# A planned order of instructions: statistics spread out, the last PSUM bank opened to dense groups, projections due earlier

## The chip, the core and the metric

The kernel runs on one core of a Trainium2 chip. Its time is device microseconds of one launch. Five engines take part: PE (matmul), ACT, DVE and POOL (element-wise work), and SP, which here only starts transfers. Each runs its own instructions in the order in which they were written; what one needs from another it waits for.

## The reference

Two kinds of layer alternate, A, B, A, B, each added to its input, on x of 2048 rows by 512 columns in bfloat16. Both A layers use the same weights, and so do both B layers.

```python
def _A_ref(x, wqkv, wo):
    H = 32; Dh = D // H; W = 256
    qkv = (x @ wqkv).reshape(B, S, 3, H, Dh)          # then q, k, v
    scores = einsum("bhqd,bhkd->bhqk", q, k) * (Dh ** -0.5)
    mask = (idx[:, None] - idx[None, :] >= 0) & (idx[:, None] - idx[None, :] < W)
    p = softmax(where(mask, scores, -1e9))
    o = einsum("bhqk,bhkd->bhqd", p, v)
    return o.transpose(0, 2, 1, 3).reshape(B, S, D) @ wo

def _B_ref(x, w1, w2):
    return maximum(x @ w1, 0) @ w2                    # Dff = 1792

x = A_x
x = x + _A_ref(layernorm(x), A_wqkv, A_wo)
x = x + _B_ref(layernorm(x), B_w1, B_w2)
x = x + _A_ref(layernorm(x), A_wqkv, A_wo)
x = x + _B_ref(layernorm(x), B_w1, B_w2)
```

So: 32 heads of 16 channels, attention over a window of 256 rows back, and a two-matrix block with relu.

## The kernel before

**Tiling.** The 2048 rows are cut into four chunks of 512 rows. A step k is one chunk of one pair of layers (A then B): k = 0 to 3 are the four chunks of the first pair, 4 to 7 of the second, and the texts below count chunks by this k. Step k does, in this order of data: statistics and normalising of x (`norm_stats`, `norm_pow`, `norm_apply`; the tile xn), a transpose to xnT, projections to K, Q and V, attention, a transpose of its output O to OT, the product with wo, the sum into x_sb, a second norm to xn2T, the product with w1 and relu to hT, the product with w2 and the sum. Transposes are DMA transposes on SP's queue, except those of the first and the last step, which PE makes.

**Projections.** K is spread with a zero for every other head into KBD (`spread_k`, two instructions per group), Q is copied to Qt, V is copied to Vst and then spread into V2f (`spread_v`, four instructions), in which a column of ones gives the softmax's sum. The zeros and ones of V2f are written once at the start (`c_v0` on POOL, `c_v` on DVE), the zero pads between the tiles of Pb as well (`pads`).

**Attention.** Units of 32 channels and up to eight blocks of 64 queries are cut into score groups. Each group is a set of small matmuls into the one score tile Sps (four banks), an exponential on ACT from there into Pb, and masks on POOL (two `affine_select` per block) or DVE (a minimum with `tri`). Then PV matmuls accumulate into acc, and DVE divides (a reciprocal and a product). Sps has one copy, so the scores of a group wait for the exponential of the group before.

**PSUM.** Four of the eight banks belong to Sps. The other four (the pool `psum`) are shared by the dense groups (projections, wo, w1, w2, made by `group`), by acc, by the PE transposes and by filler matmuls.

**The order of the work.** Nothing is ordered by hand. While the program is built, every piece is an `Op` with a key, a duration guessed for each engine that may do it, and what it depends on. A list scheduler (lines 686 to 786) plays these durations through: whenever an engine is free it takes the ready op of the lowest key (on the other engines than PE, of the lowest time of readiness plus key), books a buffer if the op needs one, and writes the instructions. What is written stays in that order on each engine (`InOrder`). The guessed durations set the order and nothing else; the chip takes its own time.

- Transfers of x and weights are ops that end at a fixed guessed time (`landed`, lines 235 to 238).
- A key of -1e5 + s ranks the score group s first on PE, -5e4 the PV groups, -10000 the product with wo; projections have as key the number of the first score group that needs them, less `wait` (line 484), and w1 and w2 the number of a later one.
- `keep` (lines 270 and 711): a dense group of key above -9000 may start only while more than one bank is free.
- Statistics have key 0 (line 280), so DVE takes them in the order in which x lands.
- When PE has nothing to do, a filler matmul on `ident` (the tile `warm`, lines 774 to 783) is written, if more than one bank is free.

After the loop stands an exact path for sums out of range, which a check at the end of the main path skips for these inputs.

Of the kernel before, what the change touches and what calls it, by code (L numbers as in the profile page):

```python
# [9 lines left out]
FP32 = mybir.dt.float32  # L10
# [3 lines left out]
ACT = mybir.ActivationFunctionType  # L14
# [48 lines left out]
def kernel(  # L63
# [32 lines left out]
    class InOrder:  # L96


        def __init__(self, eng):
            self.eng, self.last = eng, None  # L100

        def __getattr__(self, op):
            fn = getattr(self.eng, op)

            def call(*a, **k):
                inst = fn(*a, **k)  # L106
                if chained[0]:
# [143 lines left out]
    EVAC = {512: {"DVE": 0.66, "ACT": 0.59}, 256: {"DVE": 0.42, "ACT": 0.38}}  # L251
# [4 lines left out]
    def group(key, n, us, make, deps=(), item_deps=None, width=512, lead=0):  # L256

        box = Box(psum)
        box.ps = None
        last = None  # L260
        for i in range(n):
            def fn(i=i):
                if i == 0:
                    box.ps = box.tile([P, 512], FP32, "ps_d")
                make(i, box.ps)
            d = list(deps) if i == 0 else [last]
            if item_deps is not None:
                d.append(item_deps[i])
            last = op(key if i == 0 else key - lead, {"PE": (us, fn)}, d, box if i == 0 else None, [box],
                      1 if key > -9000 else 0)  # L270
        return box, last

    def norm_stats(lid, j, src, deps, eps_from=None):
        def fn():
            st = small.tile([P, 6], FP32, name="st", bufs=4)
            dve.bn_stats(out=st[:], in_=src)
            dve.bn_aggr(out=mvs[:, lid % 8, j, :], in_=st[:])
            if eps_from is not None:
                dve.tensor_scalar_add(rstds[:, lid % 8, eps_from:j + 1], mvs[:, lid % 8, eps_from:j + 1, 1], 1e-5)
        return op(0, {"DVE": (0.85 + (0.16 if eps_from is not None else 0), fn)}, deps)  # L280
# [5 lines left out]
    def norm_apply(lid, j, src, deps, by_array, dst, then_key, dst_deps):  # L286
# [12 lines left out]
        times = {"DVE": 0.46} if by_array else {"POOL": 1.15, "DVE": 0.5}  # L299
        a = op(0, options(times, fn), list(deps) + list(dst_deps), box)  # L300
# [8 lines left out]
    def transpose(key, src, dst, deps, uses, take=None):  # L309
        box = Box(psum)  # L310

        def fn():
            box.ps = box.tile([P, KC, P], BF16, "tp")
            for kc in range(KC):
                pe.transpose(box.ps[:, kc, :], src()[:, kc * P:(kc + 1) * P], ident[:])
        t = op(key, {"PE": (0.26, fn)}, deps, box, list(uses) + [box])
        return op(0, options({"DVE": 0.6, "ACT": 0.59}, lambda e: copy(e, dst(), box.ps[:])), [t], take, [box])
# [120 lines left out]
    c_v0 = [op(6, {"POOL": (0.96, lambda s0=s0: pool.memset(V2f[:, 544 * s0:544 * (s0 + 4)].bitcast(FP32), 0.0))})  # L438
# [5 lines left out]
    c_v = [op(12, {"DVE": (0.6, lambda s0=s0: v_ones(s0))}, [c_v0[s0 // 4]]) for s0 in range(0, NSLOT, 4)]  # L444
# [16 lines left out]
    def plan_qkv(k):  # L461
# [22 lines left out]
        wait = 0 if k == 0 else 8  # L484
        for h in range(2) if k == 0 else (None,):
# [5 lines left out]
            for t in range(4):  # L491
# [6 lines left out]
                times = {"DVE": 1.42, "ACT": 1.37} if h is None else {"DVE": 0.82, "ACT": 0.76}  # L498
# [15 lines left out]
        for j in range(4):  # L514
# [11 lines left out]
            v_done[k, j] = op(at, options({"POOL": 1.65, "DVE": 1.42} if k else {"POOL": 1.65, "DVE": 1.42, "ACT": 1.48}, lambda e, j=j, vs=vs: spread_v(e, layer, c, j, vs.t[:])),  # L526
# [3 lines left out]
    def plan_attention(k):  # L530
        layer, c = divmod(k, NCH)
        prev = units_of.get(k - 1, []) if c else []
        for n in units_of[k]:
# [3 lines left out]
            for g in range(len(u.groups)):  # L537
# [17 lines left out]
                for m in u.masks(g):  # L555
                    times = {"DVE": 0.32 + 0.14 * (len(m) - 1), "POOL": 0.88 * len(m)}
                    masks[s].append(op(0, options(times, lambda e, m=m, g=g, pb=pb: mask(e, m, places(pb, g))), [exps[s]] + c_tri))
            for jl in range(u.nq // 2):
# [24 lines left out]
                divs[k, u.t, j] = op(-1, {"DVE": (0.46, dfn)}, [pvs[n, jl]] + war + checks[k - 2:k - 1], None, [box])  # L583
        checks.append(op(40, {"DVE": (1.5, lambda k=k: accumulate_check(chks[k % 2], k == 0))},
# [121 lines left out]
    score_next = [0]  # L706

# [21 lines left out]
    def begin(e, t, o):  # L729
# [7 lines left out]
        us, fn, *total = o.opts[e]  # L737
        fn()
# [204 lines left out]
```

## Time and profile before

| | |
|---|---|
| runs | 504.32, 506.89, 507.78 us; median 506.89 |
| the profiled execution | 508.45 us, its span 506.4 us |
| mean granted clock of PE | 0.978 |
| busy: PE, DVE, ACT, POOL | 465.0, 363.5, 345.4, 303.0 us |
| first projection starts | 11.32 us |
| last matmul group | up to 500.8 us, then a sum on DVE and the last store |

Line numbers in the profile are nearly all L106, because every instruction passes through the helper `InOrder`; groups are told apart by their tiles. In the names, `ps_d<-xnT,wqkv` is a projection to K or Q, `ps_d<-wqkv,xnT` one to V, `ps_d<-wo,OT` the product with wo, `ps_d<-xn2T,w` and `ps_d<-w,hT` those with w1 and w2, `Sps<-Qt,KBD` scores, `acc<-V2f,Pb` PV, `tp` a transpose on PE. PEld is PE's loading of weights, which lies beside its matmuls. A bracket at the end of a row of the timeline gives the idle time of the engine before the row and what ended it.

### The profile page before, as it was taken

To read this page: it belongs to the slowest core of one execution; us is meant where nothing else is said; L and a number is where in the kernel's file an instruction comes from. 1 tells how busy PE (TensorE), PEld (TensorE's weight loads), DVE (VectorE), ACT (ScalarE), POOL (GpSimd) and SP (SyncE) were. 2 spreads that over 40 slices of the span, in tenths; PEclk is the share of its full clock that TensorE was granted. 3 is DMA by queue.
4 is the path that set the end of the run, shared out by engine and by line. 5 is a ranking of instruction groups with operands and counts; after the bars stand their busy time and mean duration, and the time that the engine had idled before them with its cause. 6 is when DMAs were issued, how large, how long until landed. Compare 5 with 4: busy or idle time off the path is not lost.

```text
span 506.4 us, 14630 instructions
## 1 busy us (share of the span) xinstructions
PE 465.0 (92%) x5989; PEld 253.8 (50%) x6064; DVE 363.5 (72%) x977; ACT 345.4 (68%) x298; POOL 303.0 (60%) x681
## 2 busy tenths in 40 slices
PE   8669899999799998999998999998999899999995
PEld 3335555655455543554444455554454554455662
DVE  5878886978778885798757976888558883586411
ACT  2747787878578876786667877886677767665340
POOL 6658866658786487646735657767547663563000
PEclk9769999999899999999999999999999999999999
DMA  8903112112130022203202201211202202000000
GB/s 268 350 8 60 25 24 23 22 24 44 23 63 3 12 46 31 43 3 43 43 1 43 43 14 32 43 13 33 53 29 48 43 3 64 23 1 13 32 22 27
DMA packets 54651, 22.00 MB, mean 43 GB/s; under 512 B 46128, under 2 KB 54064, under 8 KB 54576
## 3 DMA queue, kind: packets, MB, share of 16 engines
q1 hardware_dynamic: 54576, 20.98, 18.7%
q8 instruction: 49, 0.80, 0.7%
q14 instruction: 26, 0.21, 0.1%
HBM read 7.86 MB, written 2.10 MB: 20 GB/s over the span
## 4 chain that ended last, share of the span: by engine, by line
PE 66%; POOL 11%; DVE 6%; DMA 6%; ACT 5%; issue 4%; SPq 1%; POOLq 0%; ACTq 0%; DVEq 0%
PE ps_d L106 46%; PE acc L106 12%; PE Sps L106 8%; POOL Pb L106 6%; ACT Pb L106 4%; DMA xnT<-xn 3%; DMA x_sb<-in_A_x_dram 2%; POOL rstds L106 2%; DVE st L106 1%; POOL xn L106 1%; POOL V2f L106 1%; DVE KBD L106 1%; SPq L106 1%; DVE Pb L106 1%; DMA xn2T<-xn 1%
## 5 line engine op out<-in xcount | busy, mean ns | idle before, releaser
L106 ACT ACTIVATE Pb<-Sps 128x2048 bf16<-128x2048 f32 (+4 forms) x164 | 283.9, 1731 | 107.8 <-PE Sps L106 77.6
L106 POOL TENSOR_SCALAR_AFFINE_SELECT Pb<-Pb 64x256 bf16<-64x256 bf16 x502 | 219.5, 437 | 136.2 <-ACT Pb L106 115.5
L106 PE MATMUL ps_d<-xn2T,w 128*128 128x512 bf16 (+1 forms) x540 | 107.9, 335 | 2.4 <-issue 1.4
L106 PE MATMUL ps_d<-w,hT 128*128 128x512 bf16 x426 | 105.1, 382 | 1.7 <-issue 1.0
L106 PEld LDWEIGHTS <-Pb 128*128 128x128 bf16 x2880 | 84.8, 96 | 32.7 <-issue 9.7
L106 PE MATMUL acc<-V2f,Pb 128*128 128x34 bf16 x2880 | 91.6, 179 | 8.2 <-DVE V2f L106 4.0
L106 DVE TENSOR_TENSOR Pb<-Pb,tri 128x512 bf16<-128x512 bf16 (+1 forms) x140 | 58.6, 423 | 24.8 <-ACT Pb L106 24.1
L106 PE MATMUL Sps<-Qt,KBD 32*128 32x192 bf16 (+4 forms) x1536 | 62.8, 250 | 10.7 <-ACT Pb L106 6.1
L106 PE MATMUL ps_d<-xnT,wqkv 128*128 128x512 bf16 (+1 forms) x268 | 66.3, 367 | 4.3 <-DMA xnT<-xn 2.9
L106 PEld LDWEIGHTS <-w 128*128 128x128 bf16 x560 | 50.8, 97 | 38.3 <-issue 4.4
L106 PEld LDWEIGHTS <-hT 128*128 128x128 bf16 x448 | 40.5, 98 | 45.2 <-issue 3.2
L106 PEld LDWEIGHTS <-KBD 32*128 32x128 bf16 x1536 | 27.1, 92 | 58.2 <-issue 50.0
L106 DVE TENSOR_SCALAR hT<-ps_d 128x512 bf16<-128x512 f32 (+1 forms) x79 | 48.7, 622 | 8.3 <-PE ps_d L106 7.4
L106 DVE BATCH_NORM_STATS2 st<-x_sb 128x6 f32<-128x512 f32 (+1 forms) x64 | 43.8, 684 | 5.2 <-DMA x_sb<-in_A_x_dram 4.6
L106 DVE TENSOR_TENSOR x_sb<-ps_d,x_sb 128x512 f32<-128x512 f32 x48 | 32.6, 685 | 15.8 <-PE ps_d L106 15.7
L106 DVE RECIPROCAL chk<-acc 128x8 f32<-128x8 f32 x128 | 26.0, 203 | 24.3 <-PE acc L106 21.7
L106 PEld LDWEIGHTS <-wqkv 128*128 128x128 bf16 x288 | 26.1, 100 | 29.6 <-issue 5.2
L106 DVE TENSOR_TENSOR O<-acc,chk 128x128 bf16<-128x128 f32 x128 | 37.3, 292 | 4.6 <-DVE chk L106 0.3
L106 DVE TENSOR_SCALAR KBD<-ps_d,par 128x512 bf16<-128x512 f32 (+1 forms) x64 | 36.4, 616 | 5.2 <-PE ps_d L106 5.2
L106 ACT ACTIVATE hT<-ps_d 128x256 bf16<-128x256 f32 (+1 forms) x61 | 28.2, 466 | 13.6 <-PE ps_d L106 12.0
L106 PE MATMUL ps_d<-wo,OT 128*128 128x512 bf16 x119 | 31.9, 380 | 5.5 <-DMA OT<-O 5.0
L106 POOL TENSOR_TENSOR rstds<-rstds,mhalf 128x2 f32<-128x2 f32 (+1 forms) x33 | 24.0, 728 | 20.3 <-DVE rstds L106 17.1
(55 smaller groups left out, 292.8 us busy)
## 6 DMA issues: line engine op xcount, KB each, us to landing
w<-in_B_w_dram SPq DMA_DIRECT2D x2, 1792.0 KB, 13.6
out_dram<-ob SPq DMA_DIRECT2D x16, 128.0 KB, 1.7
wqkv<-in_A_wqkv_dram SPq DMA_DIRECT2D x3, 512.0 KB, 7.4
x_sb<-in_A_x_dram SPq DMA_DIRECT2D x3, 512.0 KB, 9.4
x_sb<-in_A_x_dram SPq DMA_DIRECT2D x2, 256.0 KB, 3.5
wo<-in_A_wo_dram SPq DMA_DIRECT2D x1, 512.0 KB, 8.9
OT<-O SPq DMA_TRANSPOSE x28, 2.5
xnT<-xn SPq DMA_TRANSPOSE x28, 2.4
```

The source lines that it names most:

```text
L106: inst = fn(*a, **k)
```

## The change

Five things in the planner are edited, and through them the order of the instructions on all engines; no instruction is computed differently.

1. Statistics get a key. `norm_stats` takes one, and step k passes -10, 6, 20 or 35 for k = 0 to 3 (else 0): the first chunk's go first, those of chunks 1 to 3 are put off. The first chunk's normalising gets key -10.
2. The memsets of V2f get keys -6 and -2 in place of 6 and 12, and the planner looks at an engine again when it first becomes free, so that constants may be placed from the start.
3. `keep` becomes 0 for all dense groups: they may take the last free bank.
4. `wait` for the projections of later steps is 16 score groups in place of 8.
5. Guessed durations and landing times are altered (DVE's and POOL's norm, masks on POOL, the copies of K and V, the division, the check).

```diff
-    d_x = [landed(5.0), landed(5.4)]
+    d_x = [landed(3.95), landed(4.5)]
...
-    d_xc = {c: landed(10.6 + 1.7 * c) for c in range(1, NCH)}
+    d_xc = {c: landed(11.4 + 1.7 * c) for c in range(1, NCH)}
...
             last = op(key if i == 0 else key - lead, {"PE": (us, fn)}, d, box if i == 0 else None, [box],
-                      1 if key > -9000 else 0)
+                      0)
...
-    def norm_stats(lid, j, src, deps, eps_from=None):
+    def norm_stats(lid, j, src, deps, eps_from=None, key=0):
...
-        return op(0, {"DVE": (0.85 + (0.16 if eps_from is not None else 0), fn)}, deps)
+        return op(key, {"DVE": (0.86 + (0.18 if eps_from is not None else 0), fn)}, deps)
...
-        times = {"DVE": 0.46} if by_array else {"POOL": 1.15, "DVE": 0.5}
-        a = op(0, options(times, fn), list(deps) + list(dst_deps), box)
+        times = {"DVE": 0.52} if by_array else {"POOL": 1.4, "DVE": 0.54}
+        a = op(-10 if lid == 0 else 0, options(times, fn), list(deps) + list(dst_deps), box)
...
-    c_v0 = [op(6, {"POOL": (0.96, lambda s0=s0: pool.memset(V2f[:, 544 * s0:544 * (s0 + 4)].bitcast(FP32), 0.0))})
+    c_v0 = [op(-6, {"POOL": (0.96, lambda s0=s0: pool.memset(V2f[:, 544 * s0:544 * (s0 + 4)].bitcast(FP32), 0.0))})
...
-    c_v = [op(12, {"DVE": (0.6, lambda s0=s0: v_ones(s0))}, [c_v0[s0 // 4]]) for s0 in range(0, NSLOT, 4)]
+    c_v = [op(-2, {"DVE": (0.6, lambda s0=s0: v_ones(s0))}, [c_v0[s0 // 4]]) for s0 in range(0, NSLOT, 4)]
...
+        calm = (-10, 6, 20, 35)[k] if k < 4 else 0
...
-            st.append(norm_stats(lid, j, src[j], came + applied.get(lid - 8, []), j - 1 if j % 2 else None))
-        pw = [norm_pow(lid, j, j + 2, [st[j], st[j + 1]], -5 if k == 0 else 0) for j in (0, 2)]
+            st.append(norm_stats(lid, j, src[j], came + applied.get(lid - 8, []), j - 1 if j % 2 else None, calm))
+        pw = [norm_pow(lid, j, j + 2, [st[j], st[j + 1]], calm - 5) for j in (0, 2)]
...
-        wait = 0 if k == 0 else 8
+        wait = 0 if k == 0 else 16
...
-                    times = {"DVE": 0.32 + 0.14 * (len(m) - 1), "POOL": 0.88 * len(m)}
+                    times = {"DVE": 0.32 + 0.14 * (len(m) - 1), "POOL": 0.93 * len(m)}
...
+    for t in busy.values():
+        push(t, None, None)
```

More of the change, by code (lines that the diff above doesn't have):

```diff
@@ L99, in __init__ @@
         def __init__(self, eng):
[L100 removed]
+            self.eng, self.last, self.made = eng, None, 0
         def __getattr__(self, op):
@@ L316, in transpose @@
         t = op(key, {"PE": (0.26, fn)}, deps, box, list(uses) + [box])
-        return op(0, options({"DVE": 0.6, "ACT": 0.59}, lambda e: copy(e, dst(), box.ps[:])), [t], take, [box])
+        return op(0, options({"DVE": 0.42, "ACT": 0.59}, lambda e: copy(e, dst(), box.ps[:])), [t], take, [box])
     def slot(layer, kb):
@@ L704 @@
             offer(o)
+    for t in busy.values():
+        push(t, None, None)
     started, score_end, idle_since, log = set(), [0.0], [1.9], []
     score_next = [0]
+    by_name = {"PE": pe, "ACT": act, "DVE": dve, "POOL": pool, "SP": sp}
     def choose(e, t):
```

12 lines of the change are left out of this document (7 added, 5 removed).

## The prediction, made before the changed kernel was run

> **What bounds the kernel now.** I began with the page: the busy shares, then the clock line.
>
> ```profile
> PE 465.0 (92%) x5989; PEld 253.8 (50%) x6064; DVE 363.5 (72%) x977; ACT 345.4 (68%) x298; POOL 303.0 (60%) x681
> ...
>
> ```
>
> PE is busy for 465.0 of 506.4 us, so what can go is 41.4 us of idle PE, the filler matmuls on `ident` (the tile called warm) counted as busy, and the time at a reduced clock, which the page puts in the first three slices. The next view is the busy time by stage, with PE first, then PEld, DVE, ACT and POOL, the granted clock, the DMA share and GB/s.
>
> ```profile
> 0.00:11.30 11.30, 8.90 (x40) 3.82 (x40) 6.90 (x24) 2.62 (x4) 8.42 (x20) 1.00 0.81 258
> ...
> 16.70:30.00 13.30, 5.03 (x51) 2.92 (x52) 10.27 (x39) 5.55 (x10) 10.55 (x23) 0.63 0.65 226
> 30.00:41.60 11.60, 10.18 (x176) 6.70 (x174) 9.49 (x32) 7.91 (x9) 6.53 (x17) 0.84 0.01 1
> 41.60:51.50 9.90, 8.22 (x113) 4.05 (x112) 7.40 (x21) 7.63 (x5) 7.88 (x19) 1.00 0.49 81
> ...
> 125.00:145.00 20.00, 15.69 (x196) 7.94 (x197) 15.83 (x42) 13.60 (x10) 16.16 (x38) 0.91 0.23 43
> ...
> 195.00:205.00 10.00, 8.28 (x127) 4.37 (x127) 3.96 (x11) 4.88 (x4) 5.59 (x13) 0.83 0.01 1
> ...
> 480.00:500.80 20.80, 20.64 (x134) 13.00 (x133) 2.09 (x4) 8.01 (x21) 0.00 (x0) 1.00 0.07 21
> 500.80:506.40 5.60, 0.00 (x0) 0.00 (x0) 0.68 (x1) 0.00 (x0) 0.00 (x0) 0.86 0.11 32
> ```
>
> Two facts carry the argument. From 16.7 to 30.0 PE works 5.03 of 13.3 us, at a mean clock of 0.63: this is the one large hole. From 480 to 500.8 PE alone runs, 20.64 of 20.80 us: the program ends on matmuls that nothing else holds up, so a microsecond saved earlier on PE's path is a microsecond off the end, and the last 5.6 us (the last store) stay. Who makes the hole is in the timeline of PE; the bracket is the idle time and who ended it.
>
> ```profile
> 11.31 0.54 PEld L106 LDWEIGHTS <-xnT 128*128 128x128 bf16 x4 [0.24 <-DMA wqkv<-in_A_wqkv_dram]
> 11.32 1.04 PE L106 MATMUL ps_d<-wqkv,xnT 128*128 128x512 bf16 x4
> ...
> 18.55 0.26 PE L106 MATMUL Sps<-Qt,KBD 32*128 32x192 bf16 x4 [1.89 <-ACT Qt L106]
> 22.60 0.35 PE L106 MATMUL Sps<-Qt,KBD 32*128 32x192 bf16 x4 [1.62 <-ACT KBD L106]
> 28.35 0.19 PE L106 MATMUL acc<-V2f,Pb 128*128 128x34 bf16 x1 [3.59 <-DVE V2f L106]
> ```
>
> Two waits are for ACT, which spreads K and copies Q; the longest is for the V operand that DVE copies. What DVE did instead is in its groups from 12.80 to 42.55 us, from its first statistics of chunk 1 to the end of its eighth division. The columns are busy time, mean ns, idle time before them; the second fence is the same stretch as a window.
>
> ```profile
> L106 DVE BATCH_NORM_STATS2 st<-x_sb 128x6 f32<-128x512 bf16 x12 | 8.1, 674 | 2.4 <-DMA x_sb<-in_A_x_dram 2.4
> L106 DVE TENSOR_SCALAR KBD<-ps_d,par 128x256 bf16<-128x256 f32 x10 | 4.3, 474 | 0.0
> ...
> L106 DVE BATCH_NORM_AGGREGATE mvs<-st 128x2 f32<-128x6 f32 x12 | 2.2, 182 | 0.4
> ...
> L106 DVE MEMSET V2f<- 64x64 bf16 x10 | 1.1, 112 | 2.5 <-issue 2.1 <-POOL Pb L106 0.3
> ```
>
> ```profile
> 12.80:42.55 29.75, 19.82 (x262) 12.16 (x263) 24.37 (x83) 17.75 (x25) 18.63 (x44) 0.77 0.43 150
> ```
>
> DVE is busy 24.37 of these 29.75 us, PE 19.82, ACT 17.75: DVE, a queue that runs in order, is the bound here. All twelve statistics of chunks 1 to 3 and the ten memsets of ones stand in it ahead of the first V copy, while attention waits.
>
> **What is moved: the first 30 us (term A).** On DVE, the stretch after the first chunk's norm has been written out; V2f is the V operand, KBD the spread keys, Qt the queries, Pb the probabilities, st the statistics, O the attention output. The kernel before has, behind the last of twelve such pairs of statistics:
>
> ```order
> L106 BN_STATS st<-x_sb 128x6
> L106 BN_AGGR mvs<-st 128x2
> L106 TENSOR_SCALAR rstds<-mvs 128x2
> L106 MEMSET V2f 64x4x16 x10
> L106 TENSOR_TENSOR Pb_103<-Pb_103,tri 128x4x64
> L106 COPY V2f<-Vst 64x16x16 x4
> L106 TENSOR_SCALAR KBD<-ps_d,par 128x4x64 x2
> L106 RECIPROCAL chk_105<-acc 128x8
> ```
>
> The changed kernel, from the middle of the first chunk's norm:
>
> ```order
> L106 TENSOR_SCALAR xn<-x_sb,mvs,rstds 128x512 x2
> L106 MEMSET V2f 64x4x16 x6
> L106 TENSOR_SCALAR KBD<-ps_d,par 128x4x64 x2
> L106 CAST Qt<-ps_d 128x256
> L106 BN_STATS st<-x_sb 128x6
> L106 BN_AGGR mvs<-st 128x2
> L106 CAST Vst<-ps_d 128x512
> L106 COPY V2f<-Vst 64x16x16 x4
> L106 TENSOR_SCALAR KBD<-ps_d,par 128x4x64 x2
> ```
>
> The memsets have gone ahead of the first keys, and one pair of statistics, not twelve, stands before the first V copy. ACT loses key work and gets a V copy, for the same reason; here is its start before, then now.
>
> ```order
> L106 ACTIVATE xnT<-tp 128x4x128 x4
> L106 ACTIVATE Vst<-ps_d 128x512
> L106 ACTIVATE KBD<-ps_d,par 128x4x64 x2
> L106 ACTIVATE Qt<-ps_d 128x256
> L106 ACTIVATE Pb_102<-Sps 128x4x192
> L106 ACTIVATE Vst<-ps_d 128x512
> L106 ACTIVATE Pb_102<-Sps 128x4x448
> ```
>
> ```order
> L106 ACTIVATE xnT<-tp 128x4x128 x4
> L106 ACTIVATE Vst<-ps_d 128x512
> L106 ACTIVATE V2f<-Vst 64x16x16 x4
> L106 ACTIVATE Pb_102<-Sps 128x4x192
> L106 ACTIVATE Qt<-ps_d 128x256
> L106 ACTIVATE Pb_102<-Sps 128x4x448
> L106 ACTIVATE KBD<-ps_d,par 128x4x64 x2
> ```
>
> The first key and query copies are DVE's now; ACT's first V copy stands ahead of its first exponential.
>
> Ahead of 11.3 us I cost the change at nothing, against its name. In the new order DVE writes its constants (the pads of Pb, a pair of ones) before the first statistics, and PE's first projection is still a V projection, which now as before needs the V part of wqkv: PE was released at 11.31 us by that transfer. Its place behind the two x transfers in SP's queue is unchanged. So an earlier norm waits there; four fewer fillers ahead of it change nothing.
>
> After 12.80 us I count what DVE holds up to its eighth division. Statistics: 8 pairs, not 12, so 4 x (8.1 + 2.2)/12 = 3.4 us less. Memsets: none, so 1.1 + 2.5 = 3.6 us less (four now stand ahead of or within the norm, six between it and the first keys, where DVE waited 2.4 us for x anyway). Keys: 12 copies, not 10, so 2 x 4.3/10 = 0.9 us more. Together 6.1 us: the eighth division can end at 36.4 us where it ended at 42.55. Not all of that need come: in a shorter stretch ACT and PE are waited for more often. The two waits for ACT above, 1.89 + 1.62 = 3.5 us, are the nearest rows to that; if all of it came back the gain would be 2.6 us. I take 1.1 us off, a third of those two waits, because ACT works 17.75 us of this stretch and has slack: **A = -5.0 us, from -6.1 to -2.6**.
>
> That time reaches PE through a chain whose length the change does not touch: the transposes of O and of chunk 1's norm on SP's queue.
>
> ```profile
> 41.56 2.61 SPq L106 DMA_TRANSPOSE OT<-O  x2
> 44.35 5.83 SPq L106 DMA_TRANSPOSE xnT<-xn  x4
> ...
> 51.46 0.82 PE L106 MATMUL ps_d<-xnT,wqkv 128*128 128x512 bf16 x3 [1.01 <-DMA xnT<-xn]
> ```
>
> From the first transpose of O to chunk 1's first projection are 9.9 us, with the same six transfers in the same order now; PE waits 1.01 us for the last of them, so this chain sets its time.
>
> The clock is the unsure part of A. Windows of the hole, same columns as above:
>
> ```profile
> 16.70:20.30 3.60, 1.49 (x23) 1.07 (x24) 3.39 (x11) 3.04 (x7) 3.09 (x7) 0.98 1.04 391
> 20.30:28.30 8.00, 2.84 (x16) 1.29 (x13) 5.26 (x24) 2.51 (x4) 7.21 (x17) 0.50 0.61 199
> 28.30:33.00 4.70, 3.29 (x61) 2.31 (x63) 3.86 (x14) 1.54 (x3) 1.08 (x3) 0.50 0.00 0
> ```
>
> After 3.6 us in which PE worked 1.49 us, the clock went to 0.50 and stayed there for 12.7 us, in which PE was busy 2.84 + 3.29 = 6.1 us. At the full clock that is about 3 us of work. I do not add these 3 us to the gain, since DVE is the bound there; they are its price if the clock falls again. [...] By the rows alone a short hole keeps the clock: from 41.60 to 51.50 us it is 1.00 with 8.22 of 9.90 us busy.
>
> **The rest of the program (term B).** The other edits change costs, a due time and the bank rule, and with them the order of all later chunks. By counts no engine gains much: POOL gets 26 more mask selects and 8 fewer norms. What can change is PE's waits; after 51.5 us they are:
>
> ```profile
> PE ps_d L106 <- DMA OT<-O: 5.0, 4, 2.0
> PE ps_d L106 <- DMA xnT<-xn: 2.9, 3, 1.2
> PE acc L106 <- POOL Pb L106: 1.7, 1, 1.7
> ```
>
> ```profile
> 141.34 1.68 PE L106 MATMUL warm<-ident 128*128 128x512 bf16 x7
> 274.85 0.59 PE L106 MATMUL ps_d<-xnT,wqkv 128*128 128x512 bf16 x2 [1.21 <-DMA xnT<-xn]
> 342.97 1.04 PE L106 MATMUL ps_d<-wo,OT 128*128 128x512 bf16 x3 [1.06 <-DMA OT<-O]
> 389.74 0.59 PE L106 MATMUL ps_d<-xnT,wqkv 128*128 128x512 bf16 x2 [0.71 <-DMA xnT<-xn]
> 401.78 1.04 PE L106 MATMUL ps_d<-wo,OT 128*128 128x512 bf16 x3 [1.23 <-DMA OT<-O]
> ```
>
> Each is a transfer that PE outran, so I counted the matmuls that stand between the producer and the user in both orders, and priced them by the page's groups.
>
> ```profile
> L106 PE MATMUL ps_d<-w,hT 128*128 128x512 bf16 x426 | 105.1, 382 | 1.7 <-issue 1.0
> ...
> L106 PE MATMUL acc<-V2f,Pb 128*128 128x34 bf16 x2880 | 91.6, 179 | 8.2 <-DVE V2f L106 4.0
> ```
>
> That is 0.247 us for a dense matmul and 0.032 us for one of the PV product (and 0.04 for a score, a small term). Projections: between the last of chunk 4 and the first of chunk 5 stand 28 dense and 72 PV matmuls, before 24 and 64, so 1.2 us more and with the scores 1.9; for chunk 7 it is 28 and 96, before 24 and 96, 1.5 us. Both exceed the waits, 1.21 and 0.71 us: -1.9. Output products: for chunk 5 there are 9 dense, before 7, for chunk 6 11, before 7: some 0.8 and 1.1 us of waits of 1.06 and 1.23; for chunks 1 and 3 there is one fewer, +0.2 each: together -1.5. The seven fillers at 141.34 are one in the new order; the transfer behind them may take back half: -0.7. The one wait for a mask on POOL, 1.7 us, came with a clock of 0.83 over 10 us, another 1.7: it hangs on a coincidence of queues that a new order may or may not repeat, so half: -1.7. Against this, a reordered program makes waits of its own; I take +2.5 us, half of the four waits for O. **B = -3.3 us**, from -8.6 (all of -1.9, -1.9, -1.4 and -3.4, nothing new) to +3 (nothing gained but new waits).
>
> **Sum.** A + B = -8.3 us: span 506.4 to 498.1. The profiled execution took 508.45 us, 2.05 outside its span, and so would take 500.1. It stood 1.56 us above the median of the runs, 506.89; on that the forecast is 498.6, say **498.5 us**.
>
> **Rivals.** *The start is not relieved.* ACT takes over: its V copy stands ahead of its first exponential, and the waits for ACT return. For it: both shorter waits of PE were ACT's. Against: ACT's 17.75 busy us of 29.75. A is then -2.6, and with half of B, -1.6, the time is 506.9 - 4.2 = 502.7: within 1%.
>
> *The clock falls anyway.* The hole shrinks but PE still works under half of some 3.6 us, and A loses its 3 us: 501.5, on the border of 1%.
>
> *PV loses its bank (slower).* With the last bank open to dense groups, a PV group finds all four taken and waits for DVE to evacuate one; behind it on PE's queue stand the next scores, so ACT waits too. One evacuation of keys by DVE is two copies of 474 ns, 0.95 us. Of the 112 PV groups after chunk 0, those with under 1.5 us of matmuls between the bank's last group and their own first matmul are 7, before 6; under 1.0 us 3, before none. So the order speaks against it. It turns the sign once these waits exceed 8.3 us, nine groups; at 15 groups and 14 us, 512.5 us.
>
> *Later holes eat the gain* is the upper end of B, A + B = -2: 505.
>
> **Chances.** Forecast 0.62 (all of it faster by over 1%, which is 5.1 us and about what a measurement tells from none); start not relieved 0.10; later holes 0.05; clock 0.13, half of it beyond 1%; PV 0.10. So faster 0.68, within 1% 0.22, slower 0.10. The range takes the lower ends of A and B, less what is unlikely to come all at once: -6.1 - 8.6 = -14.7, near 491.5; above it holds the clock and the first and last rivals, to 506, and leaves PV out.
>
> **What would show it.** In the changed profile the wait of 3.59 us for V2f should be gone, the first PV matmul should start near 22 us, the first transpose of O near 36.5 us, and chunk 1's first projection near 46.5 instead of 51.46; the clock from 16.7 to 30 us should be above 0.63. PE's waits for xnT after 200 us should be gone, those for O about 3.5 us, the one for O in chunk 1 still there. A first projection well before 11.3 us would show that my nought ahead of it was wrong; waits of PV matmuls for evacuations above 5 us in total would show that the bank rule costs more than I counted; if the start gains 5 us and the end does not, the loss lies in B.

## The result

| kernel | median, lowest to highest (us) | runs | ratio to before, 95% interval |
|---|---|---|---|
| before | 506.32, 504.32 to 507.78 | 4 | |
| after | 489.12, 487.15 to 489.35 | 4 | 0.9654, 0.9611 to 0.9697 |

The change makes the kernel faster by 3.5%. The median fell by 17.2 us, where 8.4 had been forecast, and 489.12 lies below the range. The direction was right; the size was not.

### The profile page after: what moved, and what is told of

It reads as the page before. It is cut to its first block, busy times and chain, and to the rows that moved or that the text cites. A ratio compares the mean times of both kernels' runs of the same rounds, so it can differ in the third digit from the quotient of the medians.

```text
span 485.3 us, 14586 instructions
## 1 busy us (share of the span) xinstructions
PE 456.7 (94%) x5969; PEld 248.9 (51%) x6048; DVE 362.7 (75%) x977; ACT 346.2 (71%) x297; POOL 307.1 (63%) x687
## 4 chain that ended last, share of the span: by engine, by line
PE 75%; ACT 6%; DMA 6%; DVE 6%; POOL 3%; issue 3%; SPq 0%; ACTq 0%; POOLq 0%; DVEq 0%
PE ps_d L106 54%; PE acc L106 12%; PE Sps L106 9%; ACT Pb L106 6%; DMA OT<-O 3%; DMA wqkv<-in_A_wqkv_dram 2%; DMA xnT<-xn 1%; POOL Pb L106 1%; DVE KBD L106 1%; DVE x_sb L106 1%; POOL xn L106 1%; DVE st L106 1%; DVE hT L106 1%; DMA xn2T<-xn 1%; DVE O L106 0%
## 5 line engine op out<-in xcount | busy, mean ns | idle before, releaser
L106 POOL TENSOR_SCALAR_AFFINE_SELECT Pb<-Pb 64x256 bf16<-64x256 bf16 x528 | 230.3, 436 | 107.5 <-ACT Pb L106 85.3
L106 PEld LDWEIGHTS <-Pb 128*128 128x128 bf16 x2880 | 83.6, 96 | 23.0 <-issue 7.2
L106 PE MATMUL acc<-V2f,Pb 128*128 128x34 bf16 x2880 | 89.7, 178 | 2.1 <-DVE O L106 1.0
L106 PE MATMUL ps_d<-xnT,wqkv 128*128 128x512 bf16 (+1 forms) x276 | 64.7, 355 | 2.3 <-DMA xnT<-xn 0.5
L106 DVE TENSOR_TENSOR Pb<-Pb,tri 128x256 bf16<-128x256 bf16 (+1 forms) x135 | 55.6, 417 | 10.6 <-ACT Pb L106 10.1
L106 PEld LDWEIGHTS <-KBD 32*128 32x128 bf16 x1536 | 26.0, 92 | 58.4 <-issue 53.8
L106 DVE TENSOR_SCALAR hT<-ps_d 128x512 bf16<-128x512 f32 (+1 forms) x75 | 46.3, 623 | 11.5 <-PE ps_d L106 10.9
L106 ACT ACTIVATE hT<-ps_d 128x256 bf16<-128x256 f32 (+1 forms) x65 | 30.6, 471 | 24.4 <-PE ps_d L106 22.8
L106 DVE TENSOR_SCALAR KBD<-ps_d,par 128x256 bf16<-128x256 f32 (+1 forms) x76 | 41.5, 595 | 3.3 <-PE ps_d L106 3.2
L106 DVE RECIPROCAL chk<-acc 128x8 f32<-128x8 f32 x128 | 25.9, 202 | 21.3 <-PE acc L106 19.0
L106 DVE TENSOR_TENSOR ob<-ps_d,x_sb 128x512 bf16<-128x512 f32 x16 | 11.0, 690 | 33.0 <-PE ps_d L106 33.0
## 6 DMA issues: line engine op xcount, KB each, us to landing
w<-in_B_w_dram SPq DMA_DIRECT2D x2, 1792.0 KB, 14.7
```

## The profile after

The profiled execution of after took 487.15 us (span 485.3) and was the fastest of its four; that of before, 508.45, stood above its median. The two traces differ by 21.3 us, some 4 us more than the medians, and differences read from them are a little large.

Stages of after, with the columns of the prediction's windows (PE, PEld, DVE, ACT, POOL, granted clock, DMA share, GB/s); the third row is the stretch that answers to 12.80 to 42.55 us in before. It runs from DVE's first copy of keys, which now comes ahead of the first statistics of chunk 1, to the end of DVE's eighth division:

```profile
16.70:30.00 13.30, 9.63 (x167) 6.34 (x168) 12.67 (x42) 10.99 (x16) 9.94 (x23) 1.00 0.65 226
30.00:41.60 11.60, 8.77 (x149) 5.26 (x150) 10.62 (x33) 9.19 (x8) 9.48 (x22) 1.00 0.37 59
12.30:33.77 21.47, 16.24 (x258) 10.64 (x259) 20.47 (x64) 18.53 (x25) 14.15 (x32) 1.00 0.63 216
125.00:145.00 20.00, 18.34 (x271) 9.79 (x272) 17.35 (x46) 16.26 (x13) 14.51 (x34) 0.91 0.22 41
195.00:205.00 10.00, 9.79 (x159) 5.33 (x159) 9.53 (x25) 8.43 (x7) 8.96 (x21) 1.00 0.01 2
```

The hole from 16.7 to 30 us is gone: PE works 9.63 us there, not 5.03, at a clock of 1.00, not 0.63. DVE's stretch has shrunk from 29.75 to 21.47 us, and DVE is now busy in 20.47 of it. In the two later stretches, which are the same times and not the same work, PE works 18.34 us (before 15.69) and 9.79 (8.28); the clock is still 0.91 in the first and is 1.00, not 0.83, in the second. PE's timeline of after, the rows that answer to those of before:

```profile
10.57 0.39 PE L106 MATMUL ps_d<-wqkv,xnT 128*128 128x512 bf16 x1 [0.60 <-DMA wqkv<-in_A_wqkv_dram]
...
17.32 0.26 PE L106 MATMUL Sps<-Qt,KBD 32*128 32x192 bf16 x4 [0.82 <-DVE KBD L106]
...
20.99 0.27 PE L106 MATMUL Sps<-Qt,KBD 32*128 32x192 bf16 x4 [1.22 <-ACT Pb L106]
21.18 0.77 PE L106 MATMUL acc<-V2f,Pb 128*128 128x34 bf16 x24
...
43.25 1.47 PE L106 MATMUL ps_d<-xnT,wqkv 128*128 128x512 bf16 x6 [0.52 <-DMA xnT<-xn]
```

The 3.59 us wait for V2f is gone; the longest wait left there is 1.22 us, for an exponential. The chain of transposes on SP's queue, which ends in that last row, now starts at 33.35 us:

```profile
33.35 2.62 SPq L106 DMA_TRANSPOSE OT<-O  x2
36.15 5.83 SPq L106 DMA_TRANSPOSE xnT<-xn  x4
```

From its first transpose to chunk 1's first projection are 9.9 us, as before: both moved by 8.2 us. From there to the end of PE's work the trace of before needs 449.4 us (51.46 to 500.90), that of after 436.6 (43.25 to 479.80). PE's waits in that part, first before (the largest rows of the view, of which the prediction showed three), then after:

```profile
PE ps_d L106 <- DMA OT<-O: 5.0, 4, 2.0
PE Sps L106 <- ACT Pb L106: 4.7, 13, 1.3
...
PE ps_d L106 <- DMA xnT<-xn: 2.9, 3, 1.2
PE acc L106 <- POOL Pb L106: 1.7, 1, 1.7
```

```profile
...
PE Sps L106 <- ACT Pb L106: 1.5, 7, 0.5
PE ps_d L106 <- DVE O L106: 1.4, 1, 1.4
PE ps_d L106 <- DMA OT<-O: 1.2, 2, 0.6
PE acc L106 <- DVE O L106: 1.0, 2, 0.8
PE ps_d L106 <- DMA xnT<-xn: 0.5, 1, 0.5
```

All rows but "issue" (gaps of at most 0.2 us; I put them down to matmuls whose records are missing, as 5577 are recorded beside 5648 weight loads before and 5554 beside 5630 after) sum to 16.3 us before and 7.6 us after.

## The experiments

The comparisons were made in several sets, each with its own runs of the kernel before, whose median was 505.9 to 507.0 us. A gain below is (1 - ratio) x 506.3 us. **First transpose** is the start of the first transpose of O on SP's queue in the run's trace, 41.56 us in before: it shows what the start gained. What a kernel gained beyond that, it gained later. The column comes from one trace of each kernel and is good to about 1 us: four traces with the start of before have it at 41.05 to 41.95 us, three with the start of after at 33.35 to 34.81. For two kernels, bank rule alone and after without the start's edits, it does not measure the start (the section on the bank rule says why), and their last column is left open.

| kernel | median (us) | ratio, 95% interval | gain | first transpose | gained later |
|---|---|---|---|---|---|
| after | 489.12 | 0.9654, 0.9611 to 0.9697 | 17.5 | 33.35 | 9.3 |
| start's edits alone | 489.89 | 0.9652, 0.962 to 0.9684 | 17.6 | 30.53 | 6.6 |
| statistics alone | 497.18 | 0.9818, 0.977 to 0.9867 | 9.2 | 35.38 | 3.0 |
| constants alone | 496.85 | 0.9813, 0.9764 to 0.9862 | 9.5 | 39.03 | 7.0 |
| fillers in the start's hole | 503.56 | 0.9921, 0.989 to 0.9952 | 4.0 | 40.49 | 2.9 |
| bank rule alone | 500.94 | 0.9884, 0.9841 to 0.9926 | 5.9 | 42.21 | open |
| durations alone | 501.72 | 0.9890, 0.9864 to 0.9916 | 5.6 | 40.74 | 4.8 |
| due number alone | 504.99 | 0.9949, 0.9918 to 0.9979 | 2.6 | 41.03 | 2.1 |
| after without the start's edits | 493.51 | 0.9758, 0.9738 to 0.9779 | 12.3 | 42.55 | open |
| after without the bank rule | 490.34 | 0.9671, 0.962 to 0.9722 | 16.7 | 30.68 | 5.8 |
| before, order shifted (8, 27) | 503.28 | 0.9945, 0.9923 to 0.9967 | 2.8 | 41.92 | 3.2 |
| before, order shifted (9.5, 28.5) | 505.51 | 0.9985, 0.9963 to 1.0007 | 0.8 | 41.95 | 1.2 |
| start's edits, shifted (9.5, 28.5) | 490.97 | 0.9694, 0.9648 to 0.974 | 15.5 | 30.46 | 4.4 |
| start's edits, shifted (8, 27) | 492.97 | 0.9727, 0.9678 to 0.9776 | 13.8 | 30.76 | 3.0 |
| after, shifted (9.5, 28.5) | 490.76 | 0.9684, 0.9644 to 0.9723 | 16.0 | 34.53 | 9.0 |
| before, fillers at two late waits | 508.24 | 1.0024, 0.9994 to 1.0053 | -1.2 | 41.05 | -1.7 |
| after, fillers | 488.92 | 0.9640, 0.9602 to 0.9678 | 18.2 | 34.81 | 11.5 |

### The start's edits, and their two parts

The keys of statistics, first norm and V2f's constants, the landing times and the engines' first look, put into the kernel before; the durations, the bank rule and the due number stay.

```diff
-    d_x = [landed(5.0), landed(5.4)]
+    d_x = [landed(3.95), landed(4.5)]
...
-    c_v = [op(12, {"DVE": (0.6,
+    c_v = [op(-2, {"DVE": (0.6,
...
+        calm = (-10, 6, 20, 35)[k] if k < 4 else 0
...
+    for t in busy.values():
+        push(t, None, None)
```

> The kernel before with the start's edits alone: keys of the statistics and of the first norm, keys of V2f's constants, the landing times, the engines looked at when they first become free. Theory START (the start is worth what chunk 1's first projection moved, 51.46 to 43.25 us, and is carried to the end): 506.3 - 8.2 = 498 us, first projection of chunk 1 near 43 us, waits after it as in the kernel before. Rival LATER (the end is set by waits in later chunks, which take the start back): 503 to 506 us with the same early projection. Rival CHANCE (every new order has its own waits): 494 to 502, with waits after 50 us unlike those of the kernel before.

Measured: 489.89 us, below all three forecasts and as fast as the whole change; the first transpose moved by 11.0 us, more than in the whole change:

```profile
30.53 2.61 SPq L106 DMA_TRANSPOSE OT<-O  x2
```

So the start was worth twice my term A, and 6.6 us of gain came later. Then each part by itself:

```diff
-        return op(0, {"DVE": (0.85 + (0.16 if eps_from is not None else 0), fn)}, deps)
+        return op(key, {"DVE": (0.85 + (0.16 if eps_from is not None else 0), fn)}, deps)
...
+        calm = (0, 6, 20, 35)[k] if k < 4 else 0
```

> The kernel before with one thing of the start alone: the statistics of chunks 1 to 3 are put off (keys 6, 20, 35); the constants of V2f, the landing times and the first chunk's keys stay as before. In the kernel with all edits of the start the eighth division's end, against the first statistics of chunk 1, had fallen from 42.55 to 33.77 us and the time by 17.1 us. SUM OF DVE (what I believe): DVE's order is a queue ahead of the eighth division, and each thing taken out of it gives what it took: the statistics took about 3.4 us of it, so chunk 1's first projection comes 2.5 to 4.5 us earlier (47 to 49 us in place of 51.46), and the program gains these 3 us and, since its order changes, up to 4 more: 499 to 504. ALL OR NOTHING (rival): the hole is set by the copy of V alone, for which PE's first PV matmul waits; with the constants of V2f still between, the PV matmul starts later than 26 us, the clock falls as before (a mean of 0.63 from 16.7 to 30 us), and under 1.5 us is gained at the first projection of chunk 1.

```diff
-    c_v0 = [op(6, {"POOL": (0.96,
+    c_v0 = [op(-6, {"POOL": (0.96,
...
-    c_v = [op(12, {"DVE": (0.6,
+    c_v = [op(-2, {"DVE": (0.6,
```

> The kernel before with the other thing of the start alone: the zeros and ones of V2f are written ahead of the rest (keys -6 and -2 in place of 6 and 12), the statistics stay as they were, all twelve ahead of the first copy of V. SUM OF DVE (what I believe): the ones took 3.6 us of DVE between 12.80 and 42.55 us; they leave it only in so far as DVE had idle time before 12.80 us, so chunk 1's first projection comes 2.5 to 4.5 us earlier (47 to 49 us), and the two parts alone add up to about the 9 us that all edits of the start gave there. Time 499 to 504. ALL OR NOTHING (rival): the twelve statistics still keep DVE from the copy of V, the first PV matmul starts later than 25 us, the clock falls, and under 1.5 us is gained at the first projection of chunk 1. If both parts alone gain little and all edits together 9 us, it is the hole with its clock and not the sum on DVE that decides.

Measured: 497.18 and 496.85 us. The statistics moved the first transpose by 6.2 us and chunk 1's first projection from 51.46 to 46.00, the constants by 2.5 and to 49.31. PE's row with the statistics alone:

```profile
46.00 2.36 PE L106 MATMUL ps_d<-xnT,wqkv 128*128 128x512 bf16 x6 [1.36 <-DMA xnT<-xn]
```

Neither gained under 1.5 us there, so "all or nothing" falls. The 2.5 to 4.5 us that I believed in were missed on both sides, with 5.5 and 2.2. As for the sum, 6.2 + 2.5 is 8.7 of 11.0; the rest is left for the first chunk's keys, the landing times and the engines' first look, which were not run alone. The constants alone have a price that the whole change avoids: their memsets then stand ahead of the first chunk's norm, and PE's first projection starts at 14.72 us:

```profile
9.33 0.11 DVE L106 MEMSET V2f<- 64x64 bf16 x1 [0.15 <-issue]
...
11.47 1.34 DVE L106 MEMSET Pb<- 128x640 uint32 x4 [0.18 <-issue]
12.74 1.35 DVE L106 TENSOR_SCALAR xn<-x_sb,mvs,rstds 128x512 bf16<-128x512 bf16 x4
```

Each of these memsets works 0.11 us and costs 0.37, from one start to the next. Both kernels ended faster than forecast for them (499 to 504): the statistics by what they gained in the start, the constants by 7.0 us that they gained later.

### The clock in the hole

The kernel before with 28 fillers more and nothing else moved:

```diff
+    FILL = {61: 7, 72: 6, 81: 15}
...
+            n = FILL.get(pe_ops[0], 0)
...
+                for _ in range(n):
+                    mm(ps[:], ident[:], ident[:].rearrange("p (o q) -> p o q", o=1).to_broadcast([P, 4, P]), True, True)
```

> The kernel before, every instruction in its old place on every engine, with 28 filler matmuls on ident more in the hole of the start: 7 ahead of the scores that waited 1.89 us, 6 ahead of those that waited 1.62 us, 15 ahead of the first PV matmul, which waited 3.59 us; at 0.2155 us each they fit in these waits. Nothing on DVE's path changes, only whether PE is busy in the hole, and so its clock. DVE IS THE BOUND (my prediction): the clock stays near 1.00 but chunk 1's first projection stays within 1 us of 51.46, and the program gains under 1.5 us (504 to 506.5): the 8.2 us that the whole change gained up to there came from DVE's order. CLOCK (rival): from 20 to 35 us PE was busy 9.3 us by the windows at a clock of 0.5 to 0.77, of which about 3.6 us is lost clock; with the clock kept, chunk 1's first projection comes 2.5 to 4.5 us earlier (47 to 49 us), and the program gains 2.5 to 4.5 us (501.5 to 503.5): the sum of my prediction was short by the clock that it left out.

Windows of this kernel, and its PE at the end of the hole:

```profile
16.70:30.00 13.30, 10.07 (x81) 5.18 (x80) 10.25 (x40) 5.39 (x10) 10.32 (x23) 1.00 0.66 232
30.00:41.60 11.60, 10.15 (x172) 6.68 (x174) 10.42 (x34) 8.98 (x9) 7.55 (x20) 1.00 0.01 1
```

```profile
24.84 3.40 PE L106 MATMUL warm<-ident 128*128 128x512 bf16 x15
28.30 0.18 PE L106 MATMUL acc<-V2f,Pb 128*128 128x34 bf16 x1
...
50.41 0.82 PE L106 MATMUL ps_d<-xnT,wqkv 128*128 128x512 bf16 x3 [0.41 <-DMA xnT<-xn]
```

With a clock of 1.00 up to 41.6 us, the first PV matmul still starts at 28.30 us (28.35 in before), and both the first transpose and the first projection come 1.05 us earlier (the first projection is at 51.44 to 51.94 us in four traces with the start of before). So at the start DVE was the bound, as forecast, and the clock is 1.0 of the 8.2 us. DVE's only copy of a V projection in this stretch shows where: it waited 1.8 us for PE, now 0.8. The time fell by 4.0 us all the same (2.4 to 5.6 by the interval), which my theory had at under 1.5 and the rival at 2.5 to 4.5: 2.9 us came after the first transpose, in an order that is unchanged on every engine. In the two traces PE's waits behind chunk 1's first projection sum to 16.3 us in before and to 12.9 here. So one execution differs from another by some 3 us in this sum with the same order; what these 2.9 us are was not settled.

### Bank rule, durations and due number

Each of the three alone, put into the kernel before:

```diff
-                      1 if key > -9000 else 0)
+                      0)
```

> The kernel before with the bank rule alone (dense groups may take the last free PSUM bank). By the prediction it is worth nothing: 505 to 507 us. Rival BANK (the 9 us that the whole change gained beyond the start come from fuller use of the banks): about 498 us, PE's idle time after 50 us some 7 us lower. Rival PV (PV groups wait for banks): above 508 us.

```diff
-        times = {"DVE": 0.46} if by_array else {"POOL": 1.15, "DVE": 0.5}
+        times = {"DVE": 0.52} if by_array else {"POOL": 1.4, "DVE": 0.54}
...
-                    times = {"DVE": 0.32 + 0.14 * (len(m) - 1), "POOL": 0.88 * len(m)}
+                    times = {"DVE": 0.32 + 0.14 * (len(m) - 1), "POOL": 0.93 * len(m)}
```

> The kernel before with the altered guesses of durations alone (norms, masks on POOL, copies of K and V, division, check). Theory: costs alone reorder but aim at nothing, so 506 us within 3. Rival COSTS (better guesses remove the late masks and divisions that PE waited for, 1.7 us for POOL and as much for the clock, and the late transfers of O, 5.0 us): 498 to 501 us with PE's waits for POOL and O nearly gone.

```diff
-        wait = 0 if k == 0 else 8
+        wait = 0 if k == 0 else 16
```

> The kernel before with the projections due 16 score groups ahead in place of 8, alone. By the prediction's term for the transfers (xnT 1.9 us and O 1.9 us of waits covered) 502.5 us, with the waits for xnT after 200 us gone. Rival CHANCE: anywhere from 500 to 508, with other waits in their place.

All three together, which is the kernel after with the start's lines taken back:

```diff
-        calm = (-10, 6, 20, 35)[k] if k < 4 else 0
...
-    c_v = [op(-2, {"DVE": (0.6,
+    c_v = [op(12, {"DVE": (0.6,
```

> The changed kernel without the start's edits: bank rule, due time and costs alone. Theory START (the start carries the change, the other three overlap with it): the hole from 16.7 to 30 us is back, 499 to 503 us. Rival SUM (the single gains of the three, 6.1 + 2.0 + 5.3 us, add up): 493.6 us. Rival NOTHING: 506 us.

And the kernel after with the bank rule alone taken back:

```diff
-                      0)
+                      1 if key > -9000 else 0)
```

> The kernel after with the bank rule alone undone: dense groups leave one bank free again. Alone on the kernel before, the rule gained 5.4 to 6 us, of which some 2.8 up to the end of the start. BANK (rival to my prediction): it is worth something on top of the rest, and without it the time is 492 to 495. COVERED: it relieved the same hole as the start's edits, and with the hole gone it is worth nothing: 488 to 491. My prediction had priced the rule at nothing and a harm from it at 0.10.

Each edit alone is faster, by 0.5 to 1.2%. The bank rule and the durations end between two of their forecasts each. The due number ends where CHANCE had it: the waits for xnT after 200 us are gone, and two others for xnT, 1.1 us in all, have come before. The sum of the three gains, 5.9 + 5.6 + 2.6 = 14.1 us, agrees with the 12.3 of all three without the start, as the rival SUM had it (493.6).

With the bank rule in the kernel before, the chain on SP's queue is turned round: chunk 1's transposes go ahead of those of O. These are the rows of the bank rule alone, and PE's first projection of chunk 1:

```profile
36.87 5.25 SPq L106 DMA_TRANSPOSE xnT<-xn  x4
42.21 2.54 SPq L106 DMA_TRANSPOSE OT<-O  x2
```

```profile
43.97 1.47 PE L106 MATMUL ps_d<-xnT,wqkv 128*128 128x512 bf16 x5
```

The projection is 7.5 us earlier than in before, and 7.6 (43.83) with all three edits, while the first transpose of O is later; so neither marker alone tells what the start gained. Counted by the matmuls done up to 60 us without the fillers (an estimate, since some records are missing: up to 51.46 us of before 413 matmuls stand beside 417 weight loads), these two kernels are some 3.0 and 3.5 us ahead of before and after is 9.8. Most of their gain comes later, then, but not all.

On top of the start's edits the three add nothing: 17.5 against 17.6 us. Two amounts cancel there. The start is 2.8 us slower with them (33.35 against 30.53), and the bank rule is the cause, since without it after has 30.68. What comes later is 2.7 us more. The waits of PE behind chunk 1's first projection, summed as above, were 16.3 us in before, 12.4 with the start's edits alone, some 7 with the other three alone and 7.6 with all. But before has only about 12 and 14 in the two shifted orders of the next section, and so have the start's edits. So the other three edits take some 5 to 7 us of waits away, with the start's edits or without; that the start's edits took any is not shown. What the two groups do share is lost clock: span x (1 - clock), over all runs, is 9.8 us in before, 2.3 with the start's edits, 5.4 with the other three and 3.5 with all. How much of the missing gain that explains was not settled. The bank rule is worth 5.9 us alone and 1.2 in the whole, within its error.

### Is the later gain luck of the order?

The products with w1 and w2 get other due numbers, 8 and 27 or 9.5 and 28.5 in place of 9 and 28, which reorders everything from the second half of chunk 1 on and has no other meaning.

```diff
-                d0, d1 = base[k + 1] + 9, base[k + 1] + 28
+                d0, d1 = base[k + 1] + 8, base[k + 1] + 27
```

> The kernel before, with the products with w1 and w2 due one score group earlier (8 and 27 in place of 9 and 28): an edit that aims at nothing. The first 120 us of the order are as before, what follows is another order. Theory ORDER (the order of the kernel before happens to hold two costly waits, at 128 and 199 us, with the clock lowered behind each; a new order loses at least the second): 500 to 505 us. Rival NEUTRAL (such edits move the time by noise only): 506 to 508 us.

> The kernel before, with the products with w1 and w2 due half a score group later (9.5 and 28.5): aims at nothing, changes the order from about 125 us on. Theory ORDER: 500 to 505 us, the wait of 1.66 us for POOL at 199 us and the lowered clock behind it gone. Rival NEUTRAL: 506 to 508 us.

> The changed kernel with the products with w1 and w2 due half a score group later: aims at nothing. Theory ORDER: the changed order has few costly waits left, so a new one is no better: 488 to 493 us. Rival NEUTRAL: 489 within 1.

> The kernel with the start's edits alone (489.9 us), its w1 and w2 products given due numbers of 9.5 and 28.5 groups in place of 9 and 28, which changes the order from the second half of chunk 1 on and nothing before. This asks whether the 6 us that the start's edits gain after the start are more than luck of the order: the kernel before moved by -1.0 and -3.7 us under such neutral changes, the kernel after by +1.6. CHANCE (what I believe): the start's edits alone had a lucky order behind a real gain of 9 us, and another order takes 492 to 497. CAUSE (rival): something that the start leaves behind (later chunks' norms and projections further ahead of their use) makes the whole rest faster, and any order behind it takes 488 to 491.

> The same with due numbers of 8 and 27. CHANCE: 492 to 497, and not the same as the other shifted one. CAUSE: 488 to 491, as the start's edits alone. With the two shifted ones of the kernel before (503.3 and 505.5) and the unshifted pair (506 and 489.9) this gives the gain of the start's edits over three orders each: CHANCE has it near 9 to 13 us in the mean, CAUSE near 15 to 17.

Such a shift moves the time by some 1 to 3 us (489.89 to 492.97). Over three orders each, the kernel before gains 0, 3.2 and 1.2 us later, mean 1.5; the start's edits 6.6, 4.4 and 3.0, mean 4.7. One shifted run of the start's edits fell on the side of CAUSE and one on that of CHANCE; of the other three, 503.28 and 490.76 are where ORDER had them, and 505.51 lies between ORDER and NEUTRAL. So about half of the start's 6.6 us is the luck of two orders, and 3.2 us remain, which a scatter of this size neither proves nor excludes. About 1 us of these is clock: over all their runs the three kernels with the start's edits lost 1.6 us of clock on average, the three orders of before 9.4, of which 6.8 in the start by the profile of before, so some 2.6 later.

### Fillers at later waits

As in the start's hole, 9 and 7 fillers in the kernel before and 6 in the kernel after:

```diff
+    FILL = {568: 9, 865: 7}
...
+    FILL = {589: 1, 598: 3, 604: 2}
```

> The kernel before, every instruction in its old place, with 9 fillers more ahead of the product with wo that waited 2.04 us at 127.89 us and 7 ahead of the PV group that waited 1.66 us at 199.35 us. This takes away the two later stretches at a reduced clock (PE at 0.50 for 3.4 us each) and moves nothing else. CLOCK: each costs half of 3.4 us of a busy PE, 1.7 us, so 3.4 us in all less what other waits take back: 502.5 to 504.5. NOTHING (rival): other engines set the pace there (POOL, or the transfers of O), the time stays at 505 to 507. If CLOCK holds, 3.4 us of what the changed kernels gain over this one after the start is clock that their orders happen not to lose.

> The kernel after, every instruction in its place, with 6 fillers more: 1 and 3 ahead of two PV groups that waited 0.22 and 0.79 us at 124.02 and 126.74 us, and 2 ahead of the first product with w1 of chunk 1, which waited 0.36 us. From about 126.9 us its clock fell to 0.50 for 3.4 us, its only drop after the start. CLOCK: if the six fillers keep it up, the time falls by 1 to 1.7 us, to 487.4 to 488.2. TOO SHORT (rival): the waits are no longer than 0.8 us each, the clock falls all the same, or fillers delay the work behind them by as much as they save: 488.6 to 490.

Neither gained: the second ended where TOO SHORT had it, the first above both forecasts. In the first kernel both drops of the clock are gone from the profile, and another stands at 136 us; over its ten runs the clock was no better (mean 0.979, in the 23 runs of before beside it 0.980). In the second the drop at 126.9 us is gone and one has come at 22 us, where no instruction differs. CLOCK is not refuted by this, since the clock was not kept; the attempt failed.

## Why the prediction was right or wrong

**The bound: right.** The one hole was DVE's order. The fillers showed it: a kept clock alone moved the first projection by 1.05 us, the whole new order by 8.2, and putting off DVE's statistics alone by 5.5. The first PV matmul came at 21.18 us (forecast 22), the chain from O to xnT kept its 9.9 us, ACT kept up though it took work over (18.53 of 21.47 us).

**Term A, -5.0 us: measured -8.2, outside its range.** The step that failed is the term for waits: it had the wrong sign in this trace, because a wait that could go was left out of the count. I took 1.1 us off the counted 6.1, expecting ACT and PE to be waited for more often in a shorter stretch. The row of before that I had not weighed is DVE's own idle time:

```profile
L106 DVE CAST Vst<-ps_d 128x512 bf16<-128x512 f32 x1 | 0.7, 692 | 1.8 <-PE ps_d L106 1.8
```

This wait belonged to the hole: up to 34.13 us DVE stood at that copy for a V projection that PE, held up by its 3.59 us and then at a clock of 0.50, had yet to make. The fillers show 1.0 us of it to be clock; that the other 0.8 is PE's late start is argued, not shown. In after DVE copies an earlier V projection, at 14.24 us, and waits for nothing. So in this trace no 1.1 us came off, 1.8 came on, and the stretch also lost one copy of queries, 0.4: 5.0 + 1.1 + 1.8 + 0.4 = 8.3, where 29.75 - 21.47 is 8.28 us; the other rows cancel.

The profiled run of after was a lucky one here. In the traces of after shifted and after with fillers, whose start has the same order, the clock fell at 22 us, DVE waited 1.3 and 1.0 us in this stretch for PV matmuls, and chunk 1's first projection came at 44.71 and 44.62 us, 6.8 us earlier than in before and not 8.2. So the 1.1 us of waits do come where the clock falls, and A is beyond its range even then.

The other slip is the nought ahead of 11.3 us. I read a wait of 0.24 us for wqkv as a floor. In the three traces of after and its variants with the same start the V part released PE at 10.37 to 10.84 us: the norm had held the first projection in before, and the transfer just a little longer. PE was 0.75 us earlier.

**Term B, -3.3 us: by the medians 17.2 - 8.2 = -9.0, beyond its range.** Three steps failed. The waits of scores for exponentials, 4.7 us in the row above, second in the view, were left out; 1.5 us are left of them. The wait for O in chunk 1, 2.04 us, was expected to stay and went: the rows for O fell by 3.8 us (forecast 1.5). And two gains were halved that came nearly whole: POOL's 1.7 us with the clock at 200 us restored, another 1.7 (together 1.7 forecast), and six of the seven fillers, 1.3 (0.7). Right were the waits for xnT after 200 us, 1.9 us and all gone, and the new waits, +2.5: the rows for DVE grew by some 3 us. In sum the waits fell from 16.3 to 7.6 us, where the prediction had the first as 9.6.

Part of this is luck. Orders shifted by a neutral number have about 12 and 14 us of waits in the kernel before, and the same later order had 12.9 in another execution. So the 16.3 us of the profiled run stand some 2 to 4 us high, and of the gain by the medians some 1.5 us is the bad luck of before's own order (the mean of its three orders). The rows above show where the time went, not that each was owed to the edits.

**The bank rule at nothing: wrong alone, right on top.** Without the other edits it gains 5.9 us. The sum treated the edits as independent, and they are not: gains alone of 17.6 (the start) and 12.3 us (the other three) make 17.5 together.

**The rivals.** ACT did not take over. The clock did not fall at the start in the profiled run of after; in two other traces with the same start it did, for 1.7 us of lost clock against 6.8 in before. That rival's condition, PE at work for under half of some 3.6 us, was my reading of one row (1.49 of 3.60 us), and these two falls do not fit it: ahead of them PE worked 2.43 and 2.66 of 4 us. PV waited 1.3 us for DVE from chunk 1 on and not nine times 0.95. The bank rule does cost something, but in chunk 0, which that count left out: 2.7 us of the first transpose. Later holes did not eat the gain; the later part gained as much as the start.

**The clock.** "I do not add these 3 us" was right up to the first projection, where they were worth 1.0. In the shorter stretch it may count for more: in two traces 1.7 us of it lost at 22 us went with a first projection 1.4 us later than in the profiled run of after.

**A slip of the range.** Its lower end, 491.5, is 0.7 us below what its own terms give, 506.89 - 14.7 = 492.2.

## What to carry to other kernels

In an engine that runs its queue in order, idle time inside a stretch that you shorten is not a fixed cost that comes back: ask of each such wait whether the hole itself makes it. When an edit changes a scheduler's order, sum all rows of the waits view, the small ones too; find out how far that sum moves between executions and neutral orders (here 12 to 16 us) before crediting an edit with it; and do not add the separate gains of several edits. Before a difference of under 1% is put down to an edit of the planner, shift an unrelated number of it and see how far the time moves by itself: here up to some 3 us.

## What the runs showed of the hardware

The clock is lost in pieces. Summed over windows of 4 us, the lost share (one less the granted clock) comes to 6.8 us in the start of before and to 3.4 after it, up to the end of PE's work; in the starts of other kernels' profiles it is 0 (after, the start's edits alone, the fillers in the hole), 1.7 (after shifted, after with fillers), 1.8 (statistics alone), 5.1 (constants alone), 6.7 (durations alone) and 6.9 (due number alone), to within the rounding of the granted clock near a multiple of 1.7 us. In finer windows the clock of before is at 0.50 from 20.17 to 33.82 us, 13.65 us in one piece, and for 3.4 us each from 129.4 and from 201.1 us; that of after once, for 3.4 us from 126.9 us. Where it falls differs from run to run, with the same instructions and nearly the same work on PE. Two windows each, of after and of after shifted (9.5, 28.5), whose order is the same up to some 150 us:

```profile
18.00:22.00 4.00, 2.61 (x50) 1.72 (x48) 3.86 (x13) 3.01 (x5) 3.64 (x9) 1.00 1.05 369
22.00:26.00 4.00, 3.42 (x51) 2.03 (x52) 3.76 (x15) 3.62 (x5) 2.05 (x5) 1.00 0.75 242
```

```profile
18.00:22.00 4.00, 2.43 (x48) 1.66 (x48) 3.90 (x13) 2.99 (x5) 3.67 (x8) 1.00 1.05 374
22.00:26.00 4.00, 3.68 (x42) 1.87 (x42) 3.76 (x15) 3.01 (x4) 1.92 (x5) 0.57 0.87 279
```

PE worked 2.61 and 2.43 of 4 us, and the clock stayed in one and fell in the other. In after with fillers, which stand at 124 us and later, PE worked 2.66 us in the first of these windows, more than in after, and the clock of the second was 0.58. In these 4 us PE was never idle for longer than 1.22 us at a time in any of the three; in before it had worked 1.49 of the 3.6 us ahead of the fall. What makes the clock fall these runs do not show.

Much of the kernel's own scatter goes with that chance. In 62 runs of the kernel before, 504.2 to 511.4 us with mean clocks of 0.986 to 0.970, the time rises by 0.88 us for each microsecond of lost clock (span x (1 - clock)), with a correlation of 0.78. In the start's hole it is worth less, since PE mostly waits there (it worked 5.03 of 13.30 us): the fillers saved 6.5 us of lost clock on average over the runs, and gained 1.0 us up to chunk 1's first projection and 4.0 in all.
